# Moving the streamed operand's tiles by 8 or 16 bytes in a TensorE-bound kernel

## The chip, the cores and the metric

The kernel runs on one NeuronCore of one Trainium2 chip. Its metric is the device time of one execution in microseconds (us); the execution ends when the last row of the output has been written. The five engines are called as the profile calls them: PE is TensorE (and PEld its weight loads), DVE is VectorE, ACT is ScalarE, POOL is GpSimd, and SP issues the transfers.

## The reference

A block-causal attention is followed by two feed-forward products, all in float32. What is computed, cut to its core:

```python
scores = scale * q @ k.T                 # 4 batches x 8 heads, 576 tokens, 64 channels
scores = where(block_i >= block_j, scores, -1e9)      # blocks of 64 tokens
attn = softmax(scores);  x = (attn @ v) as [2304 tokens, 512]

h = x @ w_in                             # 512 -> 2048
x = (h * cos(h)) @ w_out                 # 2048 -> 512

h = x @ w2_in                            # 512 -> 2048
out = (maximum(h, 0) ** 2) @ w2_out      # 2048 -> 512
```

## The kernel before

**Precision.** Each float32 operand of the large products is cut into a high and a low part in a format that PE multiplies in one pass. A product is then three matmuls: high by high, high by low and low by high (`mm3`, L903). Every matmul loads its own 128x128 block of weights (the stationary operand) and streams the other operand (the moving one) past it, 256 to 512 columns of 4 bytes in each partition.

**Stages.** The first 405 us hold attention and the first half of the first feed-forward product. What this case is about comes after: three stages (`R.phase` 5, 6 and 7, called stage 0, 1 and 2 as in the loop at L1537), each over four chunks of 512 tokens and one of 256. In each stage half of a feed-forward block is done: the in-product `h = x @ w` (`quad` for a chunk of 512 tokens, seven products of half size in place of eight, and `two` for the short chunk), an elementwise function of h on ACT and DVE, and the out-product into y. Stage 0 does the second half of the first block, stages 1 and 2 the two halves of the second. In stages 0 and 1 the out-product streams 512 columns at a time (256 for the short chunk of stage 0), in stage 2 (`out_quad`) 256.

**The forms of x.** `quad` needs seven combinations (forms) of the quarters of x. Each is one tile `x0` to `x6` of 128 partitions x 1024 words, which holds the form's high and low part. `x_tile` (L1299) makes it in pool `x3`, with one buffer for each form. In stages 0 and 1 ACT writes the high part and DVE the low part (`x_parts`, L1302). Stage 1 also writes the forms of chunks 0, 4, 1 and 2 to DRAM (`xp_d`), and stage 2 reads those of chunks 0, 1, 2 and 4 back; its first chunk, chunk 3, goes on with the tiles that stage 1 left (`kept_parts`, L1316, `ROUNDS`, L1536).

**Where the tiles lie.** In-product weights (tiles `w` of the pools `wa` and `wo`) all start at a multiple of 128 bytes in their partition. Unused strips between the pools (`shim`, L607, called at L631 to L635 and L619) see to it that the forms of x, the tiles of g (the function's result, which the out-product reads) and all other operands of the three stages start 64 bytes behind a multiple of 128. So the moving operand x and the weights of the in-product are 64 bytes apart, counted modulo 128. In the out-product of stages 0 and 1 it is the same pair of places with the other operand on one of them. In stage 2 some weights of the out-product stand in tiles of other pools (`raw`, `so`, `x`), 64 bytes behind, where the stationary tiles of g stand as well, and there the distance is 0.

**The order.** A recorder holds every operation and a planner (`schedule`) with fixed costs sets the order on each engine before the program is built. The addresses play no part in it. PE's matmuls of in-products and out-products of different chunks are interleaved by it, in some stretches one by one.

Of the kernel before, what the change touches and what calls it, by code (L numbers as in the profile page):

```python
# [11 lines left out]
F32R = mybir.dt.float32r  # L12
# [6 lines left out]
PSUM = bass.MemoryType.PSUM  # L19
# [24 lines left out]
UPTO = [8, 12, 14, 16, 18]  # L44
NEG = -1000000000.0
BIG = 3.0e38
PI = 3.141592653589793
INV_2PI = 0.15915494309189535
BIAS56 = 56 * 2.0**27
# [7 lines left out]
class View:  # L57
    def __init__(self, vt, chain, ix, halves):
        self.vt, self.chain, self.ix, self.halves = vt, chain, ix, halves
# [34 lines left out]


class VTile(View):
    def __init__(self, pool, shape, dtype, tag, bufs, whole=False):
        self.pool, self.shape, self.dtype, self.tag, self.bufs = pool, shape, dtype, tag, bufs
        self.whole = whole
        n = int(np.prod(shape[1:]))  # L100
        self.grain = 32 if n >= 32 else 1
        self.full = (1 << (2 * (n // self.grain + 1))) - 1
        self.real = None
        self.users = []
        self.bank = self.banks = self.before = None
        super().__init__(self, [], np.arange(n).reshape(shape[1:]), 3)

    def alloc(self):
        if self.real is None:
            tag = self.tag if self.bank is None else f"bank{self.bank}"  # L110
            self.real = self.pool().tile(self.shape, self.dtype, tag=tag, name=self.tag, bufs=self.bufs)


class Banks:
# [30 lines left out]
class Recorder:  # L145
# [20 lines left out]
        self.kind = None  # L166
        self.phase = 0

    def tile(self, pool, shape, dtype, tag, bufs=1, whole=False):
        return VTile(pool, shape, dtype, tag, bufs, whole)  # L170

    @contextmanager
    def of(self, kind):
# [203 lines left out]
def real(v):  # L377
    return v.ap() if isinstance(v, View) else v
# [3 lines left out]
def kernel(  # L382
# [25 lines left out]
    R = Recorder()  # L408
# [15 lines left out]
    def act(out, in_, func, bias=None, scale=None, accum_out=None, after=()):  # L424
        kw = {}
        n = sum(x is not None and not isinstance(x, float) for x in (bias, scale))
        if accum_out is not None:
            n += 1
        cost = out.size / 1.2 + (50 if psum(in_) else 92) + 93 * n + (49 if out.size == 512 and func == ACTF.Relu and bias is not None else 0) + (115 if out.halves != 3 else 0)

        def fn():
            kw = {a: real(x) for a, x in (("bias", bias), ("scale", scale), ("accum_out", accum_out)) if x is not None}
            return nc.scalar.activation(real(out), real(in_), func, **kw)  # L433

        return R.op("ACT", cost, fn, [x for x in (out, accum_out) if x is not None], [in_, bias, scale], after)
# [10 lines left out]
    def stt(out, a, s, b, op0, op1):  # L446
        dve(
            out.size / 0.96 + 68,
            lambda: nc.vector.scalar_tensor_tensor(real(out), real(a), s, real(b), op0=op0, op1=op1),  # L449
            [out], [a, b], int(not psum(a) and not psum(b)),  # L450
        )
# [129 lines left out]
    class Pool:  # L581


        def __init__(self, name, **kw):
            self.name, self.kw, self.pool, self.after, self.stack = name, kw, None, (), None
# [18 lines left out]
    def later(names, **kw):  # L604
        return [Pool(n, **kw) for n in names]
# [32 lines left out]
    xs_p, tmp = opened(s1, "xs1", "tmp1")  # L638
    (sb,) = opened(att, "att", side="right")

    def T(pool, shape, dtype, tag, bufs=1):
        return R.tile(pool, shape, dtype, tag, bufs, whole=pool.kw.get("space") == PSUM)

    x_d = T(dram, [KD, 128, NT], F32, "x_d")
    y1_d = T(dram, [KD, 128, NT], F32, "y1_d")
    y_d = T(dram, [KD, 128, NT], F32, "y_d")


# [14 lines left out]
    R.op("DVE", 60, lambda: nc.vector.memset(real(minus56), -BIAS56), [minus56])  # L663
    R.op("DVE", 60, lambda: nc.vector.memset(real(halfpi), PI / 2), [halfpi])

# [10 lines left out]
    for i in range(2):  # L676
# [3 lines left out]
        whole = T(sb, [128, 128], F32, f"whole{i}")  # L680
# [22 lines left out]
    def turn(kind, *args, **kw):  # L703
        if turns[-1][0] != kind:
            turns.append((kind, []))
        o = act(*args, after=turns[-2][1], **kw)
        o.table = kind
        turns[-1][1].append(o)
# [217 lines left out]
    def in_cos(tmp, w_in, xs, g, n, together):  # L926
# [4 lines left out]
        for some in sets:  # L931
            for pair_, h in zip(some, h_banks(w_in, some, xs, n)):
# [3 lines left out]
                act(t, h, ACTF.Copy, scale=INV_2PI, bias=0.25)  # L936
                stt(r, t, -2 * PI, h, ALU.mult, ALU.add)

# [103 lines left out]
    def soft_min(e, ps, m, mn):  # L1042
# [3 lines left out]
            lambda: nc.vector.tensor_tensor_reduce(  # L1046
                out=real(e), in0=real(ps), in1=real(m), scale=-1.0, scalar=BIG, op0=ALU.add, op1=ALU.min,
                accum_out=real(mn),
# [217 lines left out]
    for group, steps in WORK:  # L1266
# [12 lines left out]
        if group == (3, 1):  # L1279
            wo_p, x3_p = later(("wo", "x3"), side="right")  # L1280
# [16 lines left out]
        return raw  # L1297

    def x_tile(j):  # L1299
        return T(x3_p, [128, 2, 2, 256], F32R, f"x{j}")  # L1300

    def x_parts(forms, keep):  # L1302

        ops = {}
        for j, x in forms:
            t = x_tile(j)
            hi, lo = t[:, 0], t[:, 1]
            hi_part(hi, x)
            lo_part(lo, x, hi)
            if keep is not None:  # L1310
                dma(keep[j], f(t).rearrange("p j k c -> p (j k c)"), 524288)
            ops[j] = hi, lo
        return ops

    @of("forms")
    def kept_parts(keep, which):  # L1316

        ops = {}
        for j in which:
            t = x_tile(j)  # L1320
            dma(f(t).rearrange("p j k c -> p (j k c)"), keep[j], 524288)
            ops[j] = t[:, 0], t[:, 1]
        return ops
# [87 lines left out]
    def turned(h):  # L1411
# [7 lines left out]
        r = T(tmp3, [128, 2, 256], F32, "s", 2)  # L1419
        stt(r, t, -2 * PI, h, ALU.mult, ALU.add)  # L1420
        turn("sin", r, r, ACTF.Sin, bias=halfpi)
# [221 lines left out]
```

## Time and profile before

| | |
|---|---|
| time, median of 3 runs | 974.85 us (972.89 to 976.98) |
| profiled execution | 974.84 us |
| its span, first to last instruction | 973.0 us |
| PE busy | 951.8 us (98%) |
| weight loads | 856.1 us (88%) |
| DVE / ACT / POOL busy | 713.8 / 602.3 / 208.3 us |
| granted TensorE clock, mean | 0.994 |

The span is 1.84 us shorter than the time of its execution. Matmuls are pipelined, and the profile models their ends, so that a matmul's own duration (some 278 ns for 256 columns) tells little: one starts long before the one ahead has ended. What a matmul costs is the time from its start to the start of the next. It can be read from the chain of waits, where a row of equal matmuls is one piece with a length and a count, and from the list in order of time, where each row has its start.

### The profile page before, as it was taken

Reading aid. Unit: us, or ns where it says so; the run is one execution under the profiler, and the core shown is the slowest. Engines: PE = TensorE matmul, PEld = TensorE weight load, DVE = VectorE, ACT = ScalarE, POOL = GpSimd, SP = SyncE. Lnnn points to the kernel's source line nnn. Section 1 sums busy time; section 2 is a strip of 40 time slices with the busy share of each in tenths; the row PEclk is TensorE's granted clock in tenths of the full one; section 3 lists DMA queues with packets and bytes.
Section 4 is the critical chain, followed back from the end, with each engine's and each line's share of the span. In section 5 each row is a group of like instructions: output and inputs, shape, how many; then the busy total and the mean of one; then the engine's idle time right before and its main releaser. Section 6 shows DMA issues by size and latency. Waiting matters only on the chain.

```text
span 973.0 us, 19283 instructions
## 1 busy us (share of the span) xinstructions
PE 951.8 (98%) x6996; PEld 856.1 (88%) x6996; DVE 713.8 (73%) x1581; ACT 602.3 (62%) x1285; POOL 208.3 (21%) x313
## 2 busy tenths in 40 slices
PE   7979999999999999999999999999999999999998
PEld 5757987889898989999989889998898899999998
DVE  5898667687877455588879797987885737659565
ACT  5787588785889575484758476767564433324222
POOL 3554243447687781000000000000000000000000
PEclk8999999999999999999999999999999999999999
DMA  6755233355656347563355899796947779535321
GB/s 184 192 150 124 67 85 84 105 153 182 176 174 206 109 134 263 200 254 93 109 173 181 317 360 327 268 352 215 358 139 240 245 256 416 194 104 195 96 73 60
DMA packets 155150, 185.29 MB, mean 190 GB/s; under 512 B 71728, under 2 KB 119856, under 8 KB 155056
## 3 DMA queue, kind: packets, MB, share of 16 engines
q1 hardware_dynamic: 155056, 184.07, 57.5%
q8 instruction: 55, 0.90, 0.4%
q14 instruction: 39, 0.32, 0.1%
HBM read 114.29 MB, written 69.73 MB: 189 GB/s over the span
## 4 chain that ended last, share of the span: by engine, by line
PE 88%; DMA 5%; DVE 3%; ACT 2%; issue 1%; POOL 1%; SPq 0%; ACTq 0%; POOLq 0%; DVEq 0%
PE y L548 37%; PE h L548 34%; PE t L566 6%; PE a L558 5%; PE s L558 4%; DMA wi_d<-so 2%; PE s L548 1%; DMA x<-xp_d 1%; DMA w<-wf_d 1%; DMA x<-x_d 1%; DVE e L1046 1%; POOL e L531 0%; DVE c L449 0%; DVE c L748 0%; DVE so L490 0%
## 5 line engine op out<-in xcount | busy, mean ns | idle before, releaser
L548 PE MATMUL h<-x,w 128*128 128x256 f32 x2304 | 315.8, 278 | 1.7 <-DVE r L442 0.9
L548 PEld LDWEIGHTS h<-x,w 128*128 128x128 f32 x2304 | 294.4, 188 | 6.5 <-DVE r L442 1.7
L548 PE MATMUL y<-gh,w 128*128 128x256 f32 (+2 forms) x832 | 214.7, 329 | 7.3 <-POOL w L467 6.6
L548 PEld LDWEIGHTS y<-gh,w 128*128 128x128 f32 x832 | 144.3, 189 | 19.0 <-POOL w L467 7.6
L548 PE MATMUL y<-gl,w 128*128 128x256 f32 (+2 forms) x416 | 135.0, 328 | 0.0
L548 PE MATMUL y<-w,gh 128*128 128x512 f32 (+1 forms) x450 | 124.0, 354 | 0.4 <-DVE gh L490 0.4
L548 PEld LDWEIGHTS y<-w,gh 128*128 128x128 f32 x450 | 78.9, 188 | 12.6 <-DVE gh L490 0.6
L433 ACT ACTIVATE e<-e,st 128x256 f32<-128x256 f32 (+4 forms) x144 | 82.9, 577 | 8.6 <-DVE st L1046 6.9
L1046 DVE CUSTOM_DVE_ANT_0 e<-s,mask 128x128 f32<-128x128 f32 (+4 forms) x160 | 71.3, 478 | 22.9 <-PE s L558 15.3
L531 POOL TENSOR_SCALAR e<-e,st 128x256 f32<-128x256 f32 (+4 forms) x116 | 73.0, 640 | 63.0 <-DVE st L1067 37.0
L548 PEld LDWEIGHTS y<-gl,w 128*128 128x128 f32 x416 | 78.5, 189 | 6.2 <-issue 0.8
L548 PE MATMUL y<-w,gl 128*128 128x256 f32 (+1 forms) x306 | 83.5, 333 | 0.0
L472 ACT ACTIVATE gh<-r 128x512 fp32r<-128x512 f32 (+1 forms) x85 | 51.3, 610 | 40.0 <-DVE r L1404 18.2
L566 PE MATMUL t<-ident,e 128*128 128x128 f32 (+1 forms) x400 | 65.1, 282 | 4.6 <-DVE e L535 2.3
L490 DVE TENSOR_TENSOR gl<-r,gh 128x512 fp32r<-128x512 f32 (+1 forms) x83 | 54.7, 664 | 15.3 <-ACT gh L472 12.4
L442 DVE TENSOR_TENSOR o<-y,o 128x512 f32<-128x512 f32 (+1 forms) x55 | 34.8, 635 | 40.2 <-PE y L548 39.1
L548 PE MATMUL h<-xs2h,w 128*128 128x320 f32 x256 | 62.0, 313 | 0.0
L566 PEld LDWEIGHTS t<-ident,e 128*128 128x128 f32 (+1 forms) x400 | 46.4, 141 | 13.8 <-POOL e L531 4.7
L501 ACT ACTIVATE r<-t 128x384 f32<-128x384 f32 (+1 forms) x95 | 49.2, 531 | 14.6 <-PE t L566 13.1
L433 ACT ACTIVATE t<-raw,minus 128x512 int32<-128x512 int8 x64 | 48.8, 762 | 14.8 <-DMA raw<-in_moe_w_out_dram 6.8
L548 PEld LDWEIGHTS y<-w,gl 128*128 128x128 f32 x306 | 50.2, 188 | 6.1
L548 PE MATMUL h<-xs1h,w 128*128 128x256 f32 x256 | 53.5, 290 | 1.2 <-POOL w L467 0.7
(172 smaller groups left out, 1838.0 us busy)
## 6 DMA issues: line engine op xcount, KB each, us to landing
wi_d<-so SPq DMA_DIRECT2D x84, 256.0 KB, 2.8
w<-wi_d SPq DMA_DIRECT2D x42, 512.0 KB, 6.3
raw<-in_moe_w_in_dram SPq DMA_DIRECT2D x32, 512.0 KB, 4.6
raw<-in_moe_w_out_dram SPq DMA_DIRECT2D x32, 512.0 KB, 4.4
xp_d<-x SPq DMA_DIRECT2D x24, 512.0 KB, 6.0
x<-xp_d SPq DMA_DIRECT2D x24, 512.0 KB, 5.7
y_d<-o SPq DMA_DIRECT2D x34, 256.0 KB, 2.6
o<-y_d SPq DMA_DIRECT2D x32, 256.0 KB, 3.8
```

The source lines that it names most:

```text
L433: return nc.scalar.activation(real(out), real(in_), func, **kw)
L442: out.size / 0.96 + 68, lambda: nc.vector.tensor_tensor(real(out), real(a), real(b), op=op), [out], [a, b],
L472: "ACT": ("ACT", n / 1.2 + 92, lambda: nc.scalar.activation(real(hi), real(x), ACTF.Copy)),
L490: lambda: nc.vector.tensor_tensor(real(lo), real(x), real(f(hi)), op=ALU.subtract), 1,
L501: "ACT": ("ACT", n / 1.2 + 50, lambda: nc.scalar.activation(real(out), real(ps), ACTF.Copy)),
L531: lambda: nc.gpsimd.tensor_scalar(real(out), real(x), real(s), 1.0, op0=ALU.mult, op1=ALU.mult),
L548: lambda: nc.tensor.matmul(real(ps), lhsT=real(lhsT), rhs=real(rhs), start=start, stop=stop, skip_group_check=True),
L558: nc.tensor.matmul(real(ps), lhsT=real(l), rhs=real(r), start=start, stop=stop, skip_group_check=True)
L566: lambda: nc.tensor.transpose(real(out), real(in_), real(ident)[0:rows, 0:rows]), [out], [in_, ident],
L1046: lambda: nc.vector.tensor_tensor_reduce(out=real(e), in0=real(ps), in1=real(m), scale=-1.0, scalar=BIG, op0=ALU.add, op1=ALU.min, accum_o ...
```

## The change

Each form of x gets a buffer of 1056 words in place of 1024, and begins a number of words into it that depends on the stage in which the tile is made: 2 words (8 bytes) in stage 0, 4 words (16 bytes) in stage 1, 30 words (120 bytes) in stage 2. Since 1056 words are 33 times 128 bytes, all forms of a stage keep one place modulo 128. Pool `x3` grows by 896 bytes and its other tiles move by multiples of 128; nothing else moves. Counted modulo 128, the forms of x begin

| | before | after | against the in-product's weights (at 0) | against the tiles of g (at 64) |
|---|---|---|---|---|
| stage 0 | 64 | 72 | 64 becomes 72 | 0 becomes 8 |
| stage 1, and the first chunk of stage 2 | 64 | 80 | 64 becomes 80 | 0 becomes 16 |
| the other chunks of stage 2 | 64 | 56 | 64 becomes 56 | 0 becomes -8 |

768 matmuls stream forms at 72, 936 at 80 and 600 at 56, as the program is built: 2304 together. The list of instructions on every engine is row for row that of before.

```diff
+X_START = 2, 4, 30
 class VTile(View):
-    def __init__(self, pool, shape, dtype, tag, bufs, whole=False):
+    def __init__(self, pool, shape, dtype, tag, bufs, whole=False, at=0, size=0):
         self.pool, self.shape, self.dtype, self.tag, self.bufs = pool, shape, dtype, tag, bufs
-        self.whole = whole
+        self.whole, self.at, self.room = whole, at, size
...
     def alloc(self):
         if self.real is None:
             tag = self.tag if self.bank is None else f"bank{self.bank}"
-            self.real = self.pool().tile(self.shape, self.dtype, tag=tag, name=self.tag, bufs=self.bufs)
+            if not self.room:
+                self.real = self.pool().tile(self.shape, self.dtype, tag=tag, name=self.tag, bufs=self.bufs)
+                return
+
+            t = self.pool().tile([self.shape[0], self.room], self.dtype, tag=tag, name=self.tag, bufs=self.bufs)
+            t = t[:, self.at:self.at + int(np.prod(self.shape[1:]))]
+            names = "abc"[:len(self.shape) - 1]
+            self.real = t.rearrange(f"p ({' '.join(names)}) -> p {' '.join(names)}", **dict(zip(names, self.shape[1:])))
...
     def x_tile(j):
-        return T(x3_p, [128, 2, 2, 256], F32R, f"x{j}")
+        return T(x3_p, [128, 2, 2, 256], F32R, f"x{j}", 1, X_START[R.phase - 5], 1056)
```

## Rows read from the trace of the kernel before

**Rows 1.** The page: busy time of each engine, its share, instructions; the clock's tenths.

```profile
PE 951.8 (98%) x6996; PEld 856.1 (88%) x6996; DVE 713.8 (73%) x1581; ACT 602.3 (62%) x1285; POOL 208.3 (21%) x313
...
PEclk8999999999999999999999999999999999999999
```

**Rows 2.** Stretches of stages 0, 1, 2: length, busy time and count of each engine.

```profile
405.40:570.00 164.60, 163.67 (x1111) 150.58 (x1110) 137.09 (x241) 107.46 (x196) 0.00 (x0) 1.00 0.60 206
...
590.00:810.00 220.00, 219.39 (x1464) 199.29 (x1464) 165.96 (x303) 128.70 (x240) 0.00 (x0) 1.00 0.78 271
...
821.70:958.70 137.00, 136.93 (x1176) 136.97 (x1177) 89.63 (x148) 44.25 (x77) 0.00 (x0) 1.00 0.40 140
```

**Rows 3.** PE by line and shape: busy us, mean ns | idle before, releasers.

```profile
L548 PE MATMUL h<-x,w 128*128 128x256 f32 x2304 | 315.8, 278 | 1.7 <-DVE r L442 0.9 <-ACT p L501 0.4 <-DMA x<-xp_d 0.2
L548 PE MATMUL y<-w,gh 128*128 128x512 f32 x288 | 91.9, 395 | 0.0
L548 PE MATMUL y<-gh,w 128*128 128x512 f32 x256 | 82.4, 392 | 0.4 <-ACT gh L472 0.4
```

**Rows 4.** The chain of waits, in-products of x: start us, length us, piece, count.

```profile
414.02 4.73 PE h L548 x40
...
445.00 9.07 PE h L548 x80
...
477.14 10.71 PE h L548 x94
...
511.40 2.83 PE h L548 x24
...
616.93 4.24 PE h L548 x36
...
672.93 7.15 PE h L548 x63
...
723.34 3.53 PE h L548 x30
...
876.66 10.88 PE h L548 x96
...
953.53 5.42 PE h L548 x46
```

**Rows 5.** The chain, out-products of stages 0 and 1 (512 columns): the same columns.

```profile
491.26 20.14 PE y L548 x88
...
728.96 19.36 PE y L548 x83
```

**Rows 6.** PE in order of time, distance 0 (stage 2): start us, length, matmuls, count.

```profile
848.31 0.88 PE L548 MATMUL y<-raw,ws 128*128 128x256 f32 x6
849.03 0.76 PE L548 MATMUL y<-x,t 128*128 128x256 f32 x5
...
871.29 0.28 PE L548 MATMUL h<-x,w 128*128 128x256 f32 x1
...
872.47 0.28 PE L548 MATMUL h<-x,w 128*128 128x256 f32 x1
```

**Rows 7.** Tile x: instructions that write or move the forms (ns min/median/max); waits.

```profile
L472 ACT ACTIVATE x<-t x34: 615/622/637, 408.8 to 729.5; 128x512 fp32r<-128x512 f32 x34
L490 DVE TENSOR_TENSOR x<-t,x x34: 681/685/692, 412.5 to 730.3; 128x512 fp32r<-128x512 f32 x34
...
DMA to landing us min/median/max: 2.7/5.7/10.9
```

**Rows 8.** Who PE waited for: us in total, times, longest.

```profile
PE h L548 <- DVE r L442: 0.9, 2, 0.6
...
PE h L548 <- DMA x<-xp_d: 0.2, 1, 0.2
```

**Rows 9.** DMA issues of the forms: count, KB each, median us to landing.

```profile
xp_d<-x SPq DMA_DIRECT2D x24, 512.0 KB, 6.0
x<-xp_d SPq DMA_DIRECT2D x24, 512.0 KB, 5.7
```

More of the change, by code (lines that the diff above doesn't have):

```diff
@@ L167, in __init__, with tile @@
         self.phase = 0
-    def tile(self, pool, shape, dtype, tag, bufs=1, whole=False):
-        return VTile(pool, shape, dtype, tag, bufs, whole)
+    def tile(self, pool, shape, dtype, tag, bufs=1, whole=False, at=0, size=0):
+        return VTile(pool, shape, dtype, tag, bufs, whole, at, size)
     @contextmanager
@@ L639, with T @@
     (sb,) = opened(att, "att", side="right")
-    def T(pool, shape, dtype, tag, bufs=1):
-        return R.tile(pool, shape, dtype, tag, bufs, whole=pool.kw.get("space") == PSUM)
+    def T(pool, shape, dtype, tag, bufs=1, at=0, size=0):
+        return R.tile(pool, shape, dtype, tag, bufs, pool.kw.get("space") == PSUM, at, size)
     x_d = T(dram, [KD, 128, NT], F32, "x_d")
```

## The prediction

> **What bounds the kernel.** I read the page first. [...] The three stages that the change touches are tighter still: PE is idle for 0.9 us of 164.6, 0.6 of 220.0 and 0.1 of 137.0 [rows 2]. There the time is the number of matmuls times what each takes from its start to the next one's, and an edit that moves no instruction acts through that alone, or through a wait that it makes.
>
> The forms of x are the moving operand of 2304 matmuls [rows 3]. The chain of waits shows what each takes, since a piece has a length and a count [rows 4]. 9.07 us for 80 are 113.4 ns, 10.88 us for 96 are 113.3; but 4.73 us for 40 are 118.3 and 5.42 us for 46 are 117.8. So the same instruction, on the same distance of 64 bytes from its weights, runs in two rhythms, a short and a long one, and whole stretches keep one of them. The chain has 28 such pieces of 20 matmuls or more between those at 414.02 and 953.53 us, not counting one with a wait in it: 1399 matmuls in 160.1 us, 114.5 ns on average. 16 pieces with 1039 matmuls are in the short rhythm, 9 with 269 in the long one (117.9), and 3 with 91 change within (116.0). The other 905 stand singly or in short pieces among out-products.
>
> At distance 0 a third figure shows, in stage 2. Six matmuls of which both operands lie 64 bytes behind a multiple of 128 take from 848.31 to 849.03 us, 120.0 ns each; and where x alternates with an out-product, so that x streams while a tile of g on the same place modulo 128 is loaded, ten take from 871.29 to 872.47, 118.0 ns [rows 6]. That is what speaks for a link between the two operands' places and the time: 113.4 or 117.9 at distance 64, 118 to 120 at 0. No row has a distance between, and no operand before starts anywhere but at 0 or 64.
>
> [...] The out-products of 512 columns show the same mixture: 20.14 us for 88 in stage 0 (228.9 ns), 19.36 for 83 in stage 1 (233.3) [rows 5], where twice the short rhythm would be 226.8.
>
> **The change, part by part.** It adds, removes and reorders nothing; all its terms are shifts in what an unchanged instruction takes.
>
> *x against the in-product's weights.* I first need the mean now. To the 160.1 us of the long pieces I add the 905 others at an estimate of 116 ns, between 113.4 and 120: 105.0 us, together 265.1 us or 115.1 ns each. The bounds then are: all 2304 in the short rhythm, 2304 x (115.1 - 113.4) = 3.9 us less; all in the long one, 2304 x (117.9 - 115.1) = 6.5 us more; all as at distance 0, 2304 x (120.0 - 115.1) = 11.3 us more. [...] The new distances, 72, 80 and 56, are 8 and 16 of the 64 bytes that lie between the two known cases, so distance 64 is the nearest row by far, and I take it that its two rhythms stay, with another share. The rows don't tell which of them a shift favours. A straight line between the cases would cost (119 - 115.1) x 1/8 to 1/4, 0.5 to 1.0 ns or some 1.5 us; against that, the short rhythm is the one that holds in most long pieces, and the long one's are a fifth (269 of 1399) that a better phase could take away. I choose a small gain, half of the long rhythm's share: 0.5 x 0.19 x 2304 x 4.5 ns = 1.0 us less.
>
> *x against g in stage 2.* Where the two alternate, the distance 0 becomes -8 (16 for the first chunk). These are a part of the 905. Some 180 of them, by the order of instructions, at 118.0: between 0.8 us less (113.4) and 0.4 us more (120). Eight bytes from 0 is near 0; I take 0.2 us less.
>
> *Out-products beside x.* Their addresses stay. But a stretch keeps the rhythm in which it begins, so what runs ahead of it may matter. Stage 0 has 256 matmuls of 512 columns with the high part of g and stage 1 288 [rows 3], each half as many with the low part, 384 and 432 together: all at 226.8 would be 0.8 + 2.8 = 3.6 us less; stage 0 at the 233.3 of stage 1, 1.7 us more. I take 0, since they ran in steady patterns of their own.
>
> *Who else touches the forms.* ACT writes 62 high parts at some 622 ns and DVE 62 low parts at 685 [rows 7]; I take both as unchanged, since neither engine bounds: in stages 0 and 1 DVE is busy for 137 of 165 and 166 of 220 us [rows 2]. The transfers of the forms, 24 out and 24 in, land after 6.0 and 5.7 us [rows 9], under PE's work: PE waited for one of them once, 0.2 us [rows 8]. [...]
>
> The sum is -1.0 - 0.2 = -1.2 us. Against the profiled execution's own 974.84 us (973.0 of span and 1.84 around it), which is the median of the runs to 0.01, that gives 973.6 us.
>
> **The rivals.**
>
> *The distance doesn't matter.* [...] Against it stand the 120.0 ns at distance 0 beside 113.4 at 64 for the same shape. For it: the long rhythm exists at 64 too, so the places alone don't decide. As a mechanism of this kernel: the rhythm of a stretch is set by the moment at which it begins, and the places don't enter. Chance 0.07, 974.8 us.
>
> *The short rhythm everywhere.* If a few bytes break the tie between the two rhythms for the short one, x gives 3.9 us, and the out-products that then begin in it up to 3.6 more: 967.3 to 970.9 us. For it: once in it, long pieces stay so (96 matmuls in 10.88 us). Against it: three different shifts in two directions would have to do the same. Chance 0.22. Behind it lies a far case in which the 16 lost periods shrink too, down to 955 us, for which no row speaks: 0.03.
>
> *The long rhythm everywhere* (the other side). The place is the start of each matmul of x while the next weights are loaded; the price is 4.5 ns for each that is in the short rhythm now. If 72, 80 and 56 all miss the phase that lets both streams pass, x takes 117.9 ns: 974.8 + 6.5 = 981.3 us. It ends above +0.5% from three quarters of that on, which two of three stages would nearly give. For it: a fifth of the matmuls in long pieces are in it already, and so are nearly all in-products in some stretches (616.93, 723.34, 953.53 us). Chance 0.15.
>
> *The start off a boundary costs by itself.* All operands now start at a multiple of 64 bytes; after the change none of x does. If each matmul then touches one more unit of memory, as two streams that meet in one do at distance 0, it takes 120 ns: 986.2 us. Chance 0.08. [...]
>
> **The numbers.** The forecast, two rhythms with another share, has 0.45: 971 to 977 us around 973.6. A difference of 0.5%, 4.9 us, is about what a measurement of this kernel can tell from no change; the limits are 970.0 and 979.7. Faster by more: most of the short rhythm's case and the far case, 0.17 + 0.03, and 0.02 from the forecast's lower tail, 0.22. Slower by more: 0.15 + 0.08, less what stays under three quarters (0.02), and 0.01 of the forecast's upper tail, 0.22. Within: 0.56. The range of 8 in 10 reaches down into the short rhythm's case with its out-products and up to the long one's, 968 to 982, and leaves out the far case, a part of the short rhythm's, and the case at 120 ns. The forecast's own range is 971 to 977.
>
> **What the new profile would show.** Right: rows of PE with the same counts; in the chain, pieces of x at 113.4 and at 117.9 both, with fewer of the latter; the three stages within 1 us of 164.6, 220.0 and 137.0 less their small gains; ACT's and DVE's parts of x at 622 and 685 ns; PE's waits for forms under 1 us. Wrong: pieces of x at a figure that the trace before does not have (below 113 or above 119), one stage that gains where another loses, out-products at another mean than 228.9 and 233.3, or a landing of the forms that PE waits for.

## The result, and the profile after

The kernel takes 984.19 us after the change (median of 6 runs, 982.50 to 985.78) and 974.33 before it (6 runs, 972.27 to 976.98): a ratio of 1.0103, 95% interval 1.0089 to 1.0116. The forecast of 973.6 us and its range of 968 to 982 both missed, on the side of the rivals at 981.3 and 986.2.

The page of the profiled execution after the change (983.48 us, span 981.6), its busy times and its row of the in-products that stream x, beside [rows 1, 3]:

```profile
PE 962.5 (98%) x6996; PEld 867.4 (88%) x6996; DVE 714.6 (73%) x1581; ACT 602.2 (61%) x1285; POOL 208.2 (21%) x313
...
L556 PE MATMUL h<-x,w 128*128 128x256 f32 x2304 | 325.9, 282 | 0.1
```

PE is busy for 10.7 us longer with the same 6996 matmuls, and idle for 19.1 us in place of 21.2. The difference of the spans, 8.6 us, is the 10.7 less the 2.1 by which the idle time fell. No other engine's busy time moves by more than 0.8 us. The idle time just before x's matmuls has gone from 1.7 to 0.1 us, so nothing waits for a form; the matmuls themselves cost more.

The stretches from the first to the last matmul of x in stages 0, 1 and 2 (length, then busy time and count of PE, PEld, DVE, ACT and POOL, the granted clock as a share of the full one, DMA share, GB/s), which answer to [rows 2]:

```profile
405.80:573.60 167.80, 167.75 (x1111) 154.85 (x1111) 137.78 (x242) 107.95 (x197) 0.00 (x0) 1.00 0.59 202
593.20:816.10 222.90, 222.90 (x1464) 203.40 (x1463) 165.95 (x304) 128.68 (x240) 0.00 (x0) 1.00 0.77 267
827.50:967.30 139.80, 139.80 (x1177) 139.80 (x1176) 90.59 (x148) 44.25 (x77) 0.00 (x0) 1.00 0.40 138
```

They are 3.2, 2.9 and 2.8 us longer, at the same granted clock, 1.00; PE's idle time in them was 0.9, 0.6 and 0.1 us and is now 0.05 or less. The whole loss lies here: 8.9 us, against 8.6 of the span.

The chain of waits after (start us, length us, piece, count), pieces that answer to [rows 4, 5] and one of 132 matmuls, which before was

```profile
706.71 15.01 PE h L548 x132
```

After:

```profile
445.99 9.66 PE h L556 x80
...
479.27 11.31 PE h L556 x94
...
494.14 20.16 PE y L556 x88
514.30 2.90 PE h L556 x24
...
620.91 4.27 PE h L556 x36
...
711.75 15.70 PE h L556 x132
...
734.77 19.36 PE y L556 x83
...
843.49 11.51 PE h L556 x96
...
962.09 5.52 PE h L556 x46
```

80 matmuls of stage 0 went from 113.4 to 120.8 ns each, 132 of stage 1 from 113.7 to 118.9, 96 of stage 2 from 113.3 to 119.9. Even the pieces that were in the long rhythm took on more: 36 from 117.8 to 118.6, 46 from 117.8 to 120.0. Over the pieces of 20 matmuls and more between 414 and 973 us the mean is 119.6 ns (31 pieces, 1714 matmuls, 205.06 us), where it was 114.5, and not one of them is below 117. The out-products of 512 columns beside them stand still, 229.1 and 233.3 ns. So the short rhythm is not rarer; it is gone, from all three stages.

From here on the **mean of x** is the mean time from the start of one of x's matmuls to the next matmul's start, over those after which PE did not stop, worked out from the starts in the trace. It is 115.0 ns before (the forecast's estimate was 115.1) and 119.5 after: 120.4 in stage 0, 118.7 in stage 1, 119.7 in stage 2. 2304 x 4.5 ns are 10.4 us. The out-products add 0.9 us by the same reckoning (845 of 256 columns from 116.95 to 117.8, 812 of 512 columns from 231.25 to 231.5), which makes 11.3 beside the page's 10.7.

### The profile page after: what moved, and what is told of

Same layout as the page of the kernel before. It is cut to its first block, busy times and chain, and to the rows that moved or that the text cites. A ratio compares the mean times of both kernels' runs of the same rounds, so it can differ in the third digit from the quotient of the medians.

```text
span 981.6 us, 19283 instructions
## 1 busy us (share of the span) xinstructions
PE 962.5 (98%) x6996; PEld 867.4 (88%) x6996; DVE 714.6 (73%) x1581; ACT 602.2 (61%) x1285; POOL 208.2 (21%) x313
## 4 chain that ended last, share of the span: by engine, by line
PE 92%; DVE 3%; DMA 1%; ACT 1%; POOL 1%; issue 1%; POOLq 0%; SPq 0%; ACTq 0%; DVEq 0%
PE y L556 38%; PE h L556 38%; PE t L574 6%; PE a L566 5%; PE s L566 4%; PE s L556 1%; DMA wi_d<-so 1%; DMA xp_d<-x 1%; DVE e L1054 1%; DVE c L756 0%; POOL e L539 0%; DVE c L457 0%; DVE gl L498 0%; ACT r L441 0%; ACT e L441 0%
## 5 line engine op out<-in xcount | busy, mean ns | idle before, releaser
L556 PE MATMUL h<-x,w 128*128 128x256 f32 x2304 | 325.9, 282 | 0.1
L556 PEld LDWEIGHTS h<-x,w 128*128 128x128 f32 x2304 | 304.0, 189 | 4.1 <-DVE r L450 0.5
L450 DVE TENSOR_TENSOR r<-h,p 128x512 f32<-128x512 f32 x48 | 33.0, 687 | 30.1 <-PE h L556 29.5
```

The costliest lines, as they stand in the source:

```text
L450: out.size / 0.96 + 68, lambda: nc.vector.tensor_tensor(real(out), real(a), real(b), op=op), [out], [a, b],
L556: lambda: nc.tensor.matmul(real(ps), lhsT=real(lhsT), rhs=real(rhs), start=start, stop=stop, skip_group_check=True),
```

## The experiments

Every run below but the two probes is a version of the whole kernel, with the same instructions in the same order. The first table says where its operands stand, in bytes modulo 256 (why 256, the runs say): x, then the in-product's weights in their two pools, `wa` and `wo`, 1152 of x's matmuls each. "a / b" means that the tiles alternate.

| run | x | `wa`, `wo` | mean of x, ns | ratio to before (95%) |
|---|---|---|---|---|
| before | 64 | 0, 128 | 115.0 | 1 |
| after, stages 0 / 1 / 2 | 72, 80, 56, each also + 128 | 0, 128 | 120.4 / 118.7 / 119.7 | 1.0103 (1.0089 to 1.0116) |
| e1_room | 64 / 192 | 0, 128 | 117.0 | 1.0050 (1.0035 to 1.0065) |
| e2_all32 | 96 | 32, 160 | 115.0 | 1.0018 (1.0004 to 1.0032) |
| e3_x32 | 96 / 224 | 0, 128 | 118.8 | 1.0074 (1.0059 to 1.0089) |
| e5_pool896 | 192 | 0, 128 | 116.6 | 1.0037 (1.0020 to 1.0054) |
| e6_one8 | 200 | 0, 128 | 120.2 | 1.0103 (1.0083 to 1.0124) |
| e7_both8 | 200 | 0, 136 | 120.0 | 1.0106 (1.0083 to 1.0129) |
| e8_k192 | 192 | 0, 0 | 115.8 | 1.0020 (1.0009 to 1.0032) |
| e9_one16 | 208 | 0, 128 | 118.8 | 1.0094 (1.0078 to 1.0110) |
| e10_both16 | 208 | 0, 144 | 118.3 | 1.0084 (1.0062 to 1.0107) |
| e11_one48 | 240 | 0, 128 | 116.5 | 1.0034 (1.0023 to 1.0045) |
| e13_down128 | 192 | 0, 128 | 116.5 | 1.0042 (1.0030 to 1.0055) |
| e14_down256 | 64 | 0, 128 | 115.1 | 1.0008 (0.9994 to 1.0021) |
| e15_down512 | 64 | 0, 128 | 114.9 | 1.0004 (0.9991 to 1.0016) |
| e16_down1024 | 64 | 0, 128 | 115.0 | 1.0004 (0.9990 to 1.0018) |
| e17_one8b | 72 | 0, 128 | 120.0 | 1.0104 (1.0087 to 1.0121) |
| e18_k64 | 64 | 0, 0 | 117.6 | 1.0058 (1.0043 to 1.0073) |

One piece of the chain is shown for many of them: the first 96 in a row of stage 2, of which 24 have their weights in `wo` and 72 in `wa`. Stage 2 has three such rows; each took 10.88 us before ([rows 4] has the second), and the first 11.51 after. Means over the matmuls of one pool, below, are worked out from the starts in the trace and the places in the built program.

**The room without the offset.** e1_room keeps the larger buffers and starts every form at word 0, so that x is back at 64 modulo 128.

```diff
-X_START = 2, 4, 30
+X_START = 0, 0, 0
```

> The buffers of 1056 words stay, but every form of x begins at word 0 of its buffer, so at 64 modulo 128 as before; pool x3 lies 896 bytes lower. Both theories (the start's own place, the distance to the weights) expect the time of before, 974 us within 0.3%, with x at 115.0 ns from start to start. If the larger pool or its move is the cause, it stays near 984 us.

Its piece of 96 in the chain:

```profile
839.80 11.22 PE h L556 x96
```

It lost 0.50%, about half of the change, with nothing off its old place modulo 128: 116.9 ns where it should have been 113.3, which neither theory expected. Modulo 128 isn't the whole of it. The buffers put the forms at 64 and 192 modulo 256 by turns, and those still at 64 (117.2 ns) do no better than those at 192 (116.8).

**All operands 32 bytes on.** e2_all32 moves every pool, the weights too, and so keeps the distance of 64.

```diff
-    shim(ctx, "shim1", 32)
+    shim(ctx, "shim1", 64)
...
-    shim(ctx, "shim3", 96, side="right")
+    shim(ctx, "shim3", 64, side="right")
```

> Without the change, but every pool of the three stages is moved by 32 bytes, the weights too: x begins at 96, the weights at 32, the distance stays 64. Distance theory: 974 us within 0.4%, pieces of x at 113.4 and 117.9 ns. Place theory (a start off a multiple of 64 bytes costs a matmul some 4.5 ns by itself): x slower as in the changed kernel, +10 us, and the out-products, whose operands are moved as well, up to as much again: 984 to 995 us.

The same piece:

```profile
838.99 10.88 PE h L548 x96
```

The piece and the mean are those of before, and 1.0018, whose interval begins just above 1, I take as no change. A common shift of 32 bytes costs next to nothing.

**x alone 32 bytes on.** e3_x32 is the change with 8 words in place of 2, 4 and 30: x starts at a multiple of 32 bytes, at distance 96.

```diff
-X_START = 2, 4, 30
+X_START = 8, 8, 8
```

> The change with 8 words (32 bytes) in all three stages: x begins at 96, the weights at 0, distance 96. Place theory with a unit of 64 bytes: as the changed kernel, 984 us; with a unit of 16 or 32 bytes: 974 us. Distance theory: a place half-way between 64 (115.0 ns) and 0 (118 to 120 ns): x at 117 to 120.5 ns, 979 to 987 us.

```profile
842.12 11.45 PE h L556 x96
```

That is the piece in the chain of e3_x32: 119.3 ns, on a multiple of 32 bytes. It takes the larger buffers along, whose own part (e1_room) is 1.0050; with 1.0074 the place costs on top of them (the two intervals overlap a little, but each of the four times of e3_x32 lies above all four of e1_room).

**A map by itself.** e4_map is a probe without the kernel around it: twelve matmuls, repeated, with x and weights of one tile each, from many starts.

```python
for rep in range(2):
    for dx in sorted(PLACES + FINE):
        run(dx, 0, 256, rep, 4)
```

> Computes nothing of the reference: only streams of matmuls of one moving tile and one tile of weights in the pattern of the in-product (three matmuls on a pair of high and low parts, 256 columns), 48 for each pair of places, with the moving operand at 0 to 120 modulo 128 and the weights at 0, 8, 16, 32 and 64, and some with 128 and 512 columns. Place theory: the time from start to start depends on the moving operand's place modulo 64 (or 32, or 16) alone, 113 to 118 ns at its multiples and 120 elsewhere, whatever the weights' place. Distance theory: it depends on the difference alone, so that moving 72 with weights 8 is as quick as 64 with 0, and moving 72 with weights 0 as long as 64 with -8. With 512 columns a cost by units grows to twice its size, a cost by the meeting of the two streams doesn't.

PE in order of time in e4_map (start us, length, output's name with the places, count); the cost is the next start less this one, over 48:

```profile
61.19 5.85 PE L53 MATMUL x48w0n256a<-xx,ww 128*128 128x256 f32 x48
66.87 5.91 PE L53 MATMUL x56w0n256a<-xx,ww 128*128 128x256 f32 x48
72.62 5.76 PE L53 MATMUL x60w0n256a<-xx,ww 128*128 128x256 f32 x48
78.22 5.82 PE L53 MATMUL x64w0n256a<-xx,ww 128*128 128x256 f32 x48
83.88 5.83 PE L53 MATMUL x68w0n256a<-xx,ww 128*128 128x256 f32 x48
89.55 5.96 PE L53 MATMUL x72w0n256a<-xx,ww 128*128 128x256 f32 x48
95.35 5.84 PE L53 MATMUL x80w0n256a<-xx,ww 128*128 128x256 f32 x48
101.03 5.92 PE L53 MATMUL x88w0n256a<-xx,ww 128*128 128x256 f32 x48
...
118.31 5.67 PE L53 MATMUL x112w0n256a<-xx,ww 128*128 128x256 f32 x48
123.82 5.96 PE L53 MATMUL x120w0n256a<-xx,ww 128*128 128x256 f32 x48
```

From start to start a group at 64 takes 5.66 us or 117.9 ns each, at 72 5.80 or 120.8, at 80 5.68 or 118.3, at 56 5.75 or 119.8. The three new places cost nearly what the three stages of the kernel show, 120.4, 118.7 and 119.7. But the map is no function of distance (4 bytes further, at 60, it is 116.7), it never found 113.3 at 64, where the kernel lives in it, and it found 113.3 at 112: 5.51 us are 114.8 ns over all 48, and from the thirteenth on it is 113.3. The probe's two tiles begin at 128 modulo 256, so that its 64 and 0 are 192 and 128, and its 112 and 0 are 240 and 128. The streams of 512 columns decide nothing: against 64, 72 costs 6.1 ns more there and 3.1 with 256 columns, 56 costs 2.7 and 2.0.

**The map shuffled.** e12_map2 runs each of 96 pairs of places three times, in random order, 24 matmuls each.

> Computes nothing of the reference: streams of 24 matmuls as in the first map, for the moving operand at 0 to 120 modulo 128 in steps of 8 and the weights at 0, 8, 16, 24, 32 and 64, each three times in a shuffled order, so that each begins behind another one. If a start 8 bytes off a multiple of 16 costs by itself, the mean over all distances is some 120 ns for moving operands at 8 modulo 16 and 117 to 118 for the others, with weights at multiples of 16; and the three entries of one pair of places differ where the rhythm is one of how the stream began.

PE in order of time in e12_map2, x at 0 and weights at 64 in two of its three turns, each with the stream behind it:

```profile
123.73 2.91 PE L53 MATMUL x0w64n256a<-xx,ww 128*128 128x256 f32 x24
126.47 3.05 PE L53 MATMUL x24w24n256a<-xx,ww 128*128 128x256 f32 x24
...
189.35 2.99 PE L53 MATMUL x0w64n256b<-xx,ww 128*128 128x256 f32 x24
192.18 3.06 PE L53 MATMUL x104w8n256a<-xx,ww 128*128 128x256 f32 x24
```

From start to start the first takes 2.74 us and the second 2.83; matmul by matmul the first settles at 113.3 ns, the second runs at 117.7, with the same operands, the same instructions and the same alignment. So this pair of places has two rhythms, and since only what ran ahead differs, that picks one. Other pairs show no choice: over both probes x at 64 with weights at 0 has 117.8 in all five entries, and x at 112 with weights at 0 comes down to 113.3 in all five. Over 96 entries each, with weights at multiples of 16, x on a multiple of 16 bytes averages 118.0 ns (113.3 to 120.3), and x 8 bytes off one 119.8 (116.6 to 122.1): in no entry 8 bytes off is there the short rhythm, and a place on 16 leaves it possible.

**The pool moved by 896 bytes, nothing else.** e5_pool896 undoes the offset and the larger buffers and keeps only the 896 bytes by which the change's growth of pool x3 lowers the pool's start.

```diff
-                    shim(stack, "shim4", 64, side="right")
+                    shim(stack, "shim4", 960, side="right")
```

> Without the change, but pool x3 lies 896 bytes lower, as in the run with larger buffers, and the forms keep 4096 bytes from one to the next. If it was the move of the pool that cost that run its 0.5%: 978 to 979 us. If it was the 4224 bytes from form to form (with them two forms in a row no longer have one place modulo 256, and the rhythm is set anew at each change): 974 us within 0.3%, x at 115.0 ns.

```profile
839.25 11.32 PE h L548 x96
```

The piece of 96 in the chain of e5_pool896: 117.9 ns in place of 113.3, from a move by a multiple of 128 bytes.

**How far the pool must move.** e13_down128, e14_down256, e15_down512 and e16_down1024 are the same edit with 192, 320, 576 and 1088 in place of 64 bytes.

> Without the change, pool x3 128 bytes lower: the distance stays 64 modulo 128, and is another modulo 256. If only places modulo 128 count: 974 us, 115.0 ns. If the period is 256 bytes or more: a smaller share of the short rhythm, 116.5 to 117 ns, 977 to 979 us, as with 896 bytes (128 modulo 256).

> Without the change, pool x3 256 bytes lower. With a period of 256 bytes: the time of before, 974 us, 115.0 ns; with one of 512 or more: 116 to 117 ns, 976 to 979 us.

> Without the change, pool x3 512 bytes lower. With a period of 256 or 512 bytes: the time of before, 974 us, 115.0 ns; with one of 1024 or more: 116 to 117 ns, 976 to 979 us.

> Without the change, pool x3 1024 bytes lower. With any period up to 1024 bytes: the time of before, 974 us, 115.0 ns. If it stays at 116 to 117 ns, 976 to 979 us, the share of the short rhythm is no matter of a period up to 1024 bytes, and what sets it stays open.

The piece in the chain of e13_down128:

```profile
838.58 11.32 PE h L548 x96
```

and in that of e14_down256:

```profile
837.92 10.88 PE h L548 x96
```

128 bytes cost 0.42%; 256, 512 and 1024 nothing (0.08, 0.04, 0.04%, intervals across zero). As far as these moves show, what counts of a place repeats every 256 bytes. The change's 896 bytes of growth and its buffers of 4224 bytes are odd multiples of 128, which fits the 0.50% of e1_room; the move by itself cost 0.37% in e5_pool896.

**Eight bytes with the tiles fixed.** In e6_one8 the seven forms are slices of one block, 4096 bytes apart, all 8 bytes on.

```diff
+FORMS = ["x0", "x1", "x2", "x4", "x5", "x6", "x3"]
+AT = 2
...
+            if self.tag in FORMS:
...
+                    p.block = p.pool.tile([128, 7 * 1024 + 32], self.dtype, tag="forms", name="forms", bufs=1)
+                at = AT + 1024 * FORMS.index(self.tag)
+                t = p.block[:, at:at + 1024]
+                self.real = t.rearrange("p (a b c) -> p a b c", a=2, b=2)
```

> All seven forms are slices of one block, 4096 bytes from one to the next as before, and all begin 8 bytes further on, at 72 modulo 128, in all three stages. Theory of the start (8 bytes off cost by themselves, whatever the distance from form to form): x at 119.5 to 121 ns as in stage 0 of the changed kernel, 983 to 987 us. Theory of the spacing (the changed kernel lost its time through 4224 bytes from form to form alone): 974 us within 0.4%.

The chain of e6_one8:

```profile
445.90 9.60 PE h L558 x80
...
845.52 11.59 PE h L558 x96
```

120.0 and 120.7 ns, and 1.03%, as after the change. The block is 128 bytes longer than seven forms, an odd multiple again, so this run did not yet part the two causes. e17_one8b does: the block, with shim4 at 192, so that x stands at 72 and no tile has moved modulo 256.

> All forms in one block, 4096 bytes apart, at 72 modulo 256: 8 bytes on from the places of before, and nothing else moved by 128 modulo 256. If the offset alone costs what the change did: x at 119.5 to 121 ns, 983 to 986 us. If the two causes add up, it saves the 4 us of the moved pool: 980 to 981 us, x at 117.5 to 118.5 ns.

The chain of e17_one8b:

```profile
711.58 15.94 PE h L558 x132
...
844.02 11.44 PE h L558 x96
```

1.0104: eight bytes alone, here in all three stages, cost all that the change cost. The pool moved by 128 (e6_one8, 1.0103) adds nothing to it, nor do the larger buffers of the change (1.0050 by themselves). Both causes take from the same short rhythm, which can be lost once: of x's pieces of 20 matmuls and more none is below 115.0 ns in e1_room and none below 119.2 in e17_one8b, where many had 113.3 before.

**Distance 64 again, but both operands off.** e7_both8 is e6_one8 with the weights of pool `wo` 8 bytes on as well, in a block of their own. Half of x's matmuls, 1152, are then at distance 64 again and 1152 at 72, in one kernel.

```diff
+            if self.tag == "w" and self.bufs == 7:
...
+                    p.block, p.made = p.pool.tile([128, 7 * 1024 + 64], self.dtype, tag="w", name="w", bufs=1), 0
+                at = AT + 1024 * (p.made % 7)
...
+                self.real = p.block[:, at:at + 1024].rearrange("p (a b) -> p a b", a=2)
```

> As the run with all forms 8 bytes on, and the seven weight tiles of pool wo also 8 bytes on. Half of the in-products (their weights in wo) then have the distance 64 with both operands off by 8, the other half (weights in wa) the distance 72. Distance theory: the first half at 115 ns, the second at 120, 979 to 980 us. Place theory (a start off a boundary costs by itself): both halves at 119 to 121 ns, 983 to 987 us.

The chain of e7_both8, a piece that has only `wo`'s weights (2.83 us before [rows 4]), and the piece of 96:

```profile
514.41 2.88 PE h L566 x24
...
845.94 11.51 PE h L566 x96
```

The half at distance 64 has a mean of 119.7 ns, the half at 72 of 120.2; in e6_one8, with both at 72, the same halves have 119.9 and 120.5. The distance between the operands is restored, and next to nothing comes back. The probes agree: x at 72 with weights at 8 settles at 119.8 to 121.2 ns in all four entries.

**Sixteen bytes.** e9_one16 is e6_one8 with `AT = 4`, e10_both16 is e7_both8 with `AT = 4`.

> As the run with all forms 8 bytes on in one block, but 16 bytes on: x begins at 80, the weights at 0. If what costs is a start off a unit of 16 bytes, this is aligned and goes back to 974 to 979 us (x at 115 to 117 ns); with a unit of 32 or 64 bytes, x stays at 119 to 120.5 ns, 983 to 986 us. Stage 1 of the changed kernel, which begins there, had 118.7 ns: between them, 981 to 982 us, if a start 16 bytes off costs in part.

> Forms 16 bytes on and the wo weights 16 bytes on: half of the in-products have distance 64 with both off by 16, the other half distance 80. If 16 bytes is the unit and inside aligned starts the distance decides, the first half is at 115 to 117 ns and the second at 118 to 119, 977 to 980 us; if the unit is 32 or 64 bytes, both halves are at 118 to 120, 981 to 985 us.

The piece of 96 in the chain of e9_one16:

```profile
843.32 11.45 PE h L558 x96
```

16 bytes cost 0.94 and 0.84%, by the time not to be told apart from 8 (the means of x are lower, 118.8 and 118.3 against 120.2 and 120.0). The half of e10_both16 at distance 64 has 117.8 ns, the other 118.8; in e9_one16 the same halves have 118.5 and 119.0. The distance gives back 0.7 ns of the 3.3 that this half had lost.

**A place that the map recommends.** e11_one48 is e6_one8 with `AT = 12`: 112 modulo 128, the one place at which the first map had 113.3 with the weights at 0.

> Forms 48 bytes on, at 112 modulo 128, aligned to 16 bytes: the one place of the map with weights at 0, besides 64, at which a stream ran in the short rhythm of 113.3 ns, both times. If that is the place's own doing, x is at 113.4 to 114.5 ns and the kernel at 970.5 to 973 us, better than both. If the rhythm there was the luck of how the stream began, x is at 117 to 119 ns, as other places off 64 that are aligned to 16 bytes, 978 to 982 us.

```profile
618.28 4.22 PE h L558 x36
...
650.77 4.12 PE h L558 x36
...
840.01 11.21 PE h L558 x96
```

The piece of 96 in the chain of e11_one48 takes 116.8 ns, and the kernel 0.34% more than before. But the mean hides two rhythms. The first piece of 36 has only `wa`'s weights and takes 117.2 ns, the second only `wo`'s and takes 114.4, 113.3 after its first matmuls. So it is throughout: rows of 30 and more with weights in `wo` settle at 113.3, rows of 30 and more with weights in `wa` at 117.2, and where one follows the other (84 and 84 from 792.7 us on) the rhythm changes with the weights; before, most of `wa`'s rows had 113.3. The map's 112 with 0 is 240 with 128 modulo 256, and that pair only `wo`'s half has here. So the map's 113.3 belongs to a pair of places modulo 256, and the kernel confirms it for the half that has the pair. x at 240 with all weights at 128 was not run. No run beat the kernel before.

**Which 256?** If a move of x by 128 bytes matters, is it x against its weights, or x against the other tiles? e8_k192 (shim3 at 224: `wo` and x move by 128) puts x 192 behind all in-product weights, e18_k64 (shim4 at 192 as well, which brings x back) 64 behind all of them. Before, it is 64 behind `wa` and 192 behind `wo`.

```diff
-                    shim(stack, "shim4", 64, side="right")
+                    shim(stack, "shim4", 192, side="right")
...
-    shim(ctx, "shim3", 96, side="right")
+    shim(ctx, "shim3", 224, side="right")
```

> Without the change, but pool wo lies 128 bytes lower and x3 with it: all in-product weights are then at 0 modulo 256 and all forms of x at 192, where before half of the weights were at 128 and half at 0. If a change of place modulo 256 breaks the short rhythm, the share of 113.4 ns rises from two thirds, x at 113.6 to 114.7 ns, 971 to 973.5 us. If places count modulo 128 alone: 974 us within 0.3%.

> Without the change: pool wo 128 bytes lower and x3 256 lower, so that x and g keep one place, 64 modulo 256, while the weights in wo go from 128 to 0 modulo 256. If what counts is that the moving operands share one place modulo 256: 974 us, x at 115 ns. If x's place against its weights counts: the wo half loses, as where the pool moved by 128, 975 to 978 us, x at 115.7 to 117 ns.

The piece of 96 in the chain of e18_k64:

```profile
841.11 11.31 PE h L548 x96
```

In e18_k64 x and all other tiles of the three stages stand where they stood, modulo 256; only `wo` has moved, and x lost 2.6 ns on average. So the place of the weights counts at the period of 256. But it is not only the moved pair that pays: the half with weights in `wo` went from 115.2 to 117.8 ns, and the half with weights in `wa`, of which neither operand has moved, from 114.7 to 117.4. In the piece above, the 72 matmuls of `wa` ran at 113.3 behind the 24 of `wo` and now run at 117.8 behind them. And no single distance is the good one: 64 behind all gave 117.6 (117.8 in the probes), 192 behind all, which had been expected to gain, 115.8 and 0.20% more time, and before, with one each, both halves are below either.

## Why the prediction was wrong

**The step that failed** is "distance 64 is the nearest row by far, and I take it that its two rhythms stay, with another share". They don't stay: after the change, with starts 8 and 16 bytes off, no piece of 20 matmuls or more is below 117 ns, and the kernel's mean went to 119.5. The mean of two rhythms, 115.1, was treated as a point from which a small shift leads to a near one. It was the share of stretches that had locked into a rhythm open only to some places (113.3 ns, where the 96 entries 8 bytes off in e12_map2 begin at 116.6), and the nearest place in bytes was no nearer in time. The rows had a hint: 120.0 ns for two operands on one place [rows 6], near the 120.4 and 119.7 of stages 0 and 2 now; whether for the same reason isn't shown.

**A term put at nothing.** The prediction counts places modulo 128 throughout and has no term for the larger buffers and the lower pool. They cost 0.50% by themselves (e1_room). That this did not make its miss larger still is because the 8 bytes take away the same short rhythm.

**The size.** The term was put at 1.0 us less. In the trace it is 2304 x (119.5 - 115.0) = 10.4 us more, near the bound "all as at distance 0" (11.3), which the range left out. The straight line between distance 64 and 0, "some 1.5 us", was seven times too small.

**The rivals.** "The start off a boundary costs by itself" (986.2 us, chance 0.08) came nearest. What speaks for it was not known then: with distance 64 restored and both operands 8 bytes off, 119.7 ns (e7_both8); with all else fixed, 8 bytes cost all of the 1.03% (e17_one8b). Its mechanism, one more unit of memory for each matmul, is not shown. Starts on multiples of 16 lose as well, 118.7 ns in stage 1 and 0.94% in e9_one16, and starts on multiples of 32 lose too when the distance isn't 64 (e3_x32, 118.8 ns, where the larger buffers alone have 117.0), so place and pairing both count. "The long rhythm everywhere" had the right direction, but its 117.9 ns are not what the stages took, and no run shows a phase in which both streams would pass. "The distance doesn't matter" falls with e3_x32 and e18_k64: in e18_k64 only half of the weights moved, by 128 bytes, and x's matmuls became 2.6 ns dearer. "The short rhythm everywhere" is the opposite of what came. The far case behind it, 955 us at a chance of 0.03, counts 16 lost periods in a matmul: no run shows such periods, and the shortest rhythm that x's matmuls settle in, in the kernel's runs and in the probes, is 113.3 ns.

**x against g in stage 2.** 0.2 us less was expected. In the one stretch read out, pairs that alternate went from 118.0 to 120.0 ns (after, the twelve starts from 874.56 to 876.00 us). The sign was wrong, the term small.

**What held.** The out-products were taken at 0 and came to 0.9 us more, of 11.3. ACT's and DVE's parts of a form, taken as unchanged, are; the tile x after the change (ns min/median/max, [rows 7] before):

```profile
L480 ACT ACTIVATE x<-t x34: 613/623/637, 409.2 to 735.3; 128x512 fp32r<-128x512 f32 x34
L498 DVE TENSOR_TENSOR x<-t,x x34: 678/684/693, 413.0 to 736.0; 128x512 fp32r<-128x512 f32 x34
```

Its transfers land after the same medians (the page after, [rows 9] before), and PE waits for none of them:

```profile
xp_d<-x SPq DMA_DIRECT2D x24, 512.0 KB, 6.0
x<-xp_d SPq DMA_DIRECT2D x24, 512.0 KB, 5.7
```

That the mean of x is what bounds the three stages held too: over the runs the lost time follows it. 2.0 ns in e1_room are 4.6 us by 2304 matmuls, 0.47% (measured 0.50); 2.6 ns in e18_k64 0.61% (0.58); 5.0 ns in e17_one8b 1.18% (1.04).

**What stays open.** Why a stretch locks into one rhythm and keeps it; what in the memory or in PE's reads makes 8 bytes shut the short one out; why 64 for one pool and 192 for the other beats either for both; whether a layout with the pair of 240 and 128 for every matmul would beat the kernel before. The runs show times at places, and no circuit.

## What to carry to other kernels

Where PE is idle for under 1% and each matmul loads new weights, the start of the moving tile and of the weights, modulo 256 bytes, was worth up to 1% of the time (1.03% after the change) with no instruction changed. No multiple is safe by itself: here starts on multiples of 32 (e3_x32, 0.74%) and of 64 (e13_down128, 0.42%) lost too. What kept the time was to keep both operands' places modulo 256 (moves by 256, 512 and 1024 bytes: 0.08, 0.04, 0.04%), so change buffer sizes and pool starts by multiples of 256, and look at the chain again after any such edit. Read a matmul's cost from start to start over long pieces and look at the pieces apart: a mean over two rhythms is no place from which to interpolate to an address that has no row. A short probe's rhythm can depend on what ran ahead (113.3 or 117.7 ns in e12_map2), and it speaks only for pairs of places modulo 256, of the moving tile and the weights both: its 113.3 held for the half of e11_one48 that had its pair, and not for the other.

## What was unexpected

- The same 256-column matmul on the same addresses settles at 113.3 or 117.8 ns by what ran ahead of it (x at 0 and weights at 64 in e12_map2: 113.3, 117.7, 117.8).
- In e11_one48 the same tiles of x take 113.3 ns with one pool's weights and 117.2 with the other's, next to each other in one stretch.
- Places repeat at 256 bytes, as far as these moves show: moves of the pool by 256, 512 and 1024 bytes change next to nothing (0.08, 0.04, 0.04%), 128 and 896 cost 0.42 and 0.37%.
- Causes don't add: larger buffers 0.50%, 8 bytes 1.04%, both together 1.03%.
- 128 and 512 columns in e4_map don't follow in proportion: 128 columns took some 111.7 ns at nearly every place, 512 columns 229.4 to 235.5.
